# A Fourier filter and a gated feed-forward on one core: the buffer `at` of two batches laid out by halves, and small copies moved to GpSimd

## The chip, the cores and the metric

The kernel runs on one core of a Trainium2 chip. A core has engines that each work through their own queue in order: TensorE (PE, its weight loads PEld), VectorE (DVE), ScalarE (ACT), GpSimd (POOL) and SyncE (SP, which only issues transfers). They meet through semaphores. SBUF is the on-chip memory of 128 partitions; PSUM, eight banks here, takes TensorE's results; DMA queues move data between SBUF and DRAM. The metric is the device time of the program in microseconds. Before the change it is 893.33 us, the median of three runs (893.03 to 893.96).

## The reference

Eight batches of a sequence of 3008 positions by 256 channels pass a global filter in the Fourier domain, and then a feed-forward with a product of two branches:

```
X = rfft(x, axis=1)                      # x: (8, 3008, 256)
y = irfft(X * (filt_r + 1j*filt_i), n=3008, axis=1)
t = y.reshape(24064, 256)
out = (relu(t @ w_gate) * (t @ w_val)) @ w_out    # d_ff = 1536, out: (24064, 256)
```

Inputs and output are float32. The kernel uses bf16 for most matmuls.

## The kernel before

The length is split as 3008 = 94 x 32, a position being 32 n1 + n2. The transform is made of matmuls in four stages for each batch.

Stage A is the transform over n1 (94 points, real input). For batches 0 and 1 `first_a` multiplies x (`XF`, float32) by the matrix `WA`, and ScalarE copies the result out of PSUM as bf16, in two halves h of the 256 channels. What is now indexed by frequency on the partitions and n2 along the row must be turned so that n2 lies on the partitions. `turn_a` does that with VectorE's transpose of 32 x 32 blocks, on pairs of bf16 taken as float32, and writes the buffer `ats[b]` (`at` in the profile). Batch 0 is turned in two pieces of 128x2048 float32, one for each half h. Of batch 1, half 0 goes another way: `store_half` writes it to DRAM (`Abuf`) and `load_half` reads it back, turned, with four DMAs of SP's queue into channels 0 to 127 of `at`. Half 1 is turned by VectorE in four smaller pieces of 128x512. Batches 2 to 7 take other functions (`fold_chunk` on GpSimd, `tiled_a`, `load_at_tiled`).

Stage B is the transform over n2, the filter, and the way back: `fwd` (TensorE, `F2` with `at`, into `psX`), `product` (VectorE, for some of batch 0 ScalarE's copy `xs` and then GpSimd; `tt` with the real filter `Ftr`, `uu` with the imaginary filter `Fti`), `inv` (TensorE with the tables `I2t` and `I2u`, into `psD`). For batch 0 the result goes back into `AS0`, the buffer that held stage A's result, now called D: rows 0 to 23 of its 32 rows. `turn_d` transposes all 32 rows into `dCb`. Other batches write D to DRAM (`Dbuf`).

Stage C is the transform back over k1: `item_c` multiplies `dCb` by the table `M1` (`M` in the profile) into `psY`, which is copied to `yT`, a block of 512 tokens. Rows of `M1` that answer to D's spare columns are zero.

Stage D is the feed-forward, 47 blocks of 12 steps. A step (`gv`) makes `psV` and `psG` with two matmuls each, ScalarE copies `psV` to `vsb`, VectorE makes `prod` from `psG` and `vsb`; `o_part` multiplies the products of the block before by `WoT` into `psO`. From the second block on, each step also holds four matmuls of `o_part`. Every `psV`, `psG`, `psY` takes a bank from one list of eight, in the program's order; a bank is free when its reader is done.

The order on each engine is written out by hand: each engine runs its instructions as the program lists them. Work for later batches is hung on the steps with `at_step`: batch 1's remaining `turn_a` pieces at steps 4, 11 and 14, its first `fwd` at step 16, the loads of x of batch 2 from step 6. Waits are derived from the areas of memory that instructions read and write. The first `turn_a` piece of batch 1, `turn_a(1, 1, 0, 0, 16)`, stands before the first block, and so before the first `prod` on VectorE.

`place_own` writes parts of three tables from the loaded array `tabs`: the last two groups of `I2t` and `I2u` in the upper 64 partitions, and `M1`. `place_filter` copies rows of the filters to the partitions above, seven times by SP's DMA and once by GpSimd (`Fti`, 32x3072). GpSimd issues the loads of filters and of the feed-forward's weights (`load_vg`, `load_o`).

Of the kernel before, what the change touches and what calls it, by code (L numbers as in the profile page):

```python
# [12 lines left out]
FP32 = mybir.dt.float32  # L13
BF16 = mybir.dt.bfloat16
# [17 lines left out]
NG = 24  # L32
# [3 lines left out]
def _ap(t, offset_elems, ap_list):  # L36
    return dataclasses.replace(
        t, offset=t.offset + offset_elems, ap=[list(p) for p in ap_list]
    )
# [80 lines left out]
def kernel(  # L120
# [10 lines left out]
    nc = tc.nc  # L131
    B, S_, D = x.shape
# [15 lines left out]
    sb = ctx.enter_context(tc.tile_pool(name="sb", bufs=2))  # L148
# [3 lines left out]
    def bank(name, *shape):  # L152

        i = free.pop(0)
        t = ps.tile([128, *shape], FP32, tag=f"bank{i}", bufs=1, name=name)
        held[id(t)] = i, t
        return t
# [13 lines left out]
    AS0 = pro.tile([128, 32, D], BF16)  # L171
# [4 lines left out]
    M1 = consts.tile([128, 2, N1], BF16)  # L176
# [22 lines left out]
    tabs = pro.tile([128, tab_h.shape[1]], BF16, tag="tabs", bufs=1)  # L199
# [23 lines left out]
    def place_own():  # L223

        for i, t in enumerate((I2t, I2u)):
            o = 192 + i * 128
            nc.vector.tensor_copy(t[64:, NG - 2:, :],
                                  tabs[64:, o:o + 128].rearrange("p (g n) -> p g n", g=2))
        nc.vector.tensor_copy(M1, tabs[:, 448:].rearrange("p (l n) -> p l n", l=2))

    nyq = []

# [19 lines left out]
    def place_filter(fi, a, half, copy):  # L252

        dst = FILT[fi][1]
        gs = slice(H * half, H * half + H)
        r = a * 64
        copy(dst[r + 32:r + 64, gs, :], dst[r:r + 32, gs, :])
# [5 lines left out]
    def load_vg(c0, c1):  # L263
        for (w_hbm, w_sb) in ((moe_w_val, WvT), (moe_w_gate, WgT)):
            nc.gpsimd.dma_start(w_sb[:, :, c0:c1],
                                _ap(w_hbm, c0, [[DFF, 128], [128 * DFF, 2], [1, c1 - c0]]))

    def load_o():
        for c in range(2):
            nh = NFT // 2  # L270
            nc.gpsimd.dma_start(WoT[:, c * nh:(c + 1) * nh],
                                _ap(moe_w_out, c * nh * 128 * D, [[D, 128], [128 * D, nh], [1, D]]))
# [22 lines left out]
    def turn_a(b, h, i=0, d0=0, d1=None):  # L295

        src = AS[2 * b + h][i].rearrange("p l c d -> p (l c) d").bitcast(FP32).rearrange("p n d -> p d n")
        w = src.shape[1]
        d1 = d1 or w
        dst = ats[b].bitcast(FP32).rearrange("p k d -> p d k")  # L300
        o = h * D // 4 + i * w
        nc.vector.transpose(dst[:, o + d0:o + d1, :], src[:, d0:d1, :])

    def new_at(b):
        ats[b] = sb.tile([128, 32, D], BF16, tag="at", bufs=1, name="at")

    def turn_d(h):

        src = AS0.bitcast(FP32).rearrange("p k d -> p d k")
        dst = dCb[:, 0:32, :].bitcast(FP32).rearrange("p n d -> p d n")  # L310
        d = slice(h * D // 4, h * D // 4 + D // 4)
        nc.vector.transpose(dst[:, d, :], src[:, d, :])
# [7 lines left out]
    def load_half(b):  # L320
        w = N2 * D // 2
        for q in range(4):
            nc.sync.dma_start(ats[b][32 * q:32 * q + 32, 0:NG, 0:D // 2],
                              _ap(Abuf[b], q * NG * w, [[D // 2, 32], [w, NG], [1, D // 2]]))

    fold = {}
# [56 lines left out]
    ats = {}  # L383
# [4 lines left out]
    def fwd(b, i):  # L388

        for e in range(2):  # L390
            psXs[b, i, e] = bank("psX", 2, D)
            left[b, i, e] = 2
        for m in range(2):
            for e in range(2):
                for a in range(2):
                    j = 12 * a + 2 * i + m
                    nc.tensor.matmul(psXs[b, i, e][64 * a:64 * a + 64, m],  # L397
                                     F2[64 * e:64 * e + 64, j, :],
                                     ats[b][64 * e:64 * e + 64, j, :], start=True, stop=True,
                                     tile_position=(64 * e, 64 * a))  # L400

    def product(b, i, e, k, pool=False):

# [42 lines left out]
    def first_b(amid):  # L446

        for i in range(6):
            fwd(0, i)
            on_pool = [(i, e) in POOL_U for e in range(2)]  # L450
            seq = {(0, 0): ((0, 0), (0, 1), (1, 0), (1, 1)), (0, 1): ((1, 1), (0, 0), (0, 1), (1, 0)),
                   (1, 0): ((0, 1), (1, 0), (1, 1), (0, 0)), (1, 1): ((0, 0), (1, 1), (0, 1), (1, 0))}
            for e, k in seq[tuple(map(int, on_pool))]:
                product(0, i, e, k, pool=k == 1 and on_pool[e])
            if i > 1:
                inv(0, i - 2)
            amid(i)
        inv(0, 4)
        amid(6)
        inv(0, 5)  # L460
# [107 lines left out]
    q = NX2 * D // 4  # L568
# [29 lines left out]
    for i in range(3):  # L598
        make_back_u(i)
    new_at(0)  # L600
    for h in range(2):
        turn_a(0, h)
    place_own()
    for i in range(6):
        warm(2)
    place_filter(1, 0, 0, nc.gpsimd.tensor_copy)
    nc.gpsimd.memset(AS0[:, NG:, :], 0.0)
    for fi, a, half in ((0, 0, 0), (0, 1, 0), (1, 1, 0), (0, 0, 1), (0, 1, 1), (1, 0, 1), (1, 1, 1)):
        place_filter(fi, a, half, nc.sync.dma_start)
    load_x(1, sp, ((0, 0, 2 * q), (0, 2 * q, 4 * q), (1, 0, 2 * q), (1, 2 * q, 4 * q)))  # L610
# [11 lines left out]
    load_vg(0, DFF // 2)  # L622
    load_vg(DFF // 2, DFF)
    load_o()
    for h in range(2):
        turn_d(h)
    new_at(1)
    for p, s, h in items:
        first_a(1, p, s, h)
        if (p, s, h) == (3, 1, 0):  # L630
            store_half(1)
            load_half(1)
        if (p, s, h) == (3, 0, 1):
            for hh in range(2):
                item_c(0, hh)
    turn_a(1, 1, 0, 0, 16)
    nc.sync.dma_start(WF, nc.inline_tensor(fold_h, name="dft_fold").ap())
    prologue.close()
# [8 lines left out]
    for k in range(1, 4):  # L647
        at_step((4, 11, 14)[k - 1], lambda k=k: turn_a(1, 1, k // 2, k % 2 * 16, k % 2 * 16 + 16))
    for b in range(1, B):
        end = (b * S // W - 1) * NFT + C_AT[0] - 5  # L650
        if b > 1:
            for j, e in enumerate((-74, -69, -64, -57)):
                l = (6, 14, 22, 30)[j] if b == 2 else end - 115 + NFT * j

                def next_x(b=b, j=j, l=l):
                    hold_gpsimd(prods[-1][:, 0:8])
                    load_chunk(b, j)
                    if j:
                        fold_chunk(b, j - 1)
                    if j == 3:  # L660
                        fold_chunk(b, j)
                at_step(l, next_x)
                at_step(end + e, lambda b=b, j=j: tiled_a(b, j))
            at_step(end + e + 4, lambda b=b: load_at_tiled(b))
        for i in range(7):
            l = -35 + 5 * i if b == 1 else -40 + 6 * i
            if i < 6:
                at_step(end + l, lambda b=b, i=i: fwd(b, i))
                for h in range(4):
                    at_step(end + l + h, lambda b=b, i=i, h=h: product(b, i, h // 2, h % 2))  # L670
            if i > 0:
                at_step(end + l, lambda b=b, i=i: inv(b, i - 1))
        at_step(end - 2, lambda b=b: load_d(b))
# [42 lines left out]
```

## Time and profile before

| | |
|---|---|
| Median of three runs | 893.33 us |
| The profiled execution's own time | 893.89 us |
| Its span, first to last instruction | 892.1 us |
| TensorE busy | 866.5 us, 97% of the span |
| VectorE, ScalarE, GpSimd busy | 65%, 56%, 41% |
| Mean granted TensorE clock | 0.994 |
| Moved by DMA | 102.87 MB, mean 115 GB/s |

A profile row of the order of time reads: start in us from the span's first instruction, duration in us, engine, line, operation, out<-in, shapes, number of merged instructions, and in brackets the idle time of the engine before it and what ended that. A row of waits reads: who waited for whom, us in total, times, the longest. A row of groups has count, busy us and mean ns. Matmuls overlap, so their starts tell more than their durations. A DMA's landing is told from its issue. The granted clock is a share of TensorE's full clock.

### The profile page before, as it was taken

To read this page: it belongs to the slowest core of one execution; us is meant where nothing else is said; L and a number is where in the kernel's file an instruction comes from. 1 tells how busy PE (TensorE), PEld (TensorE's weight loads), DVE (VectorE), ACT (ScalarE), POOL (GpSimd) and SP (SyncE) were. 2 spreads that over 40 slices of the span, in tenths; PEclk is the share of its full clock that TensorE was granted. 3 is DMA by queue.
4 is the path that set the end of the run, shared out by engine and by line. 5 is a ranking of instruction groups with operands and counts; after the bars stand their busy time and mean duration, and the time that the engine had idled before them with its cause. 6 is when DMAs were issued, how large, how long until landed. Compare 5 with 4: busy or idle time off the path is not lost.

```text
span 892.1 us, 19099 instructions
## 1 busy us (share of the span) xinstructions
PE 866.5 (97%) x7072; PEld 509.0 (57%) x7193; DVE 579.6 (65%) x864; ACT 501.3 (56%) x905; POOL 365.3 (41%) x365
## 2 busy tenths in 40 slices
PE   8869999999999999999999999999999999999997
PEld 4325555566556665566655566556655566666665
DVE  3847766577665776667766677657776577655553
ACT  5644655556655556555655556555665555555553
POOL 6805980038841488216690167802886000000001
PEclk9989999999999999999999999999999999999999
DMA  9893436534466436463375434763456513331111
GB/s 242 226 160 95 108 102 154 122 86 124 129 143 134 115 100 144 128 142 93 100 174 130 103 100 108 184 125 89 116 142 148 121 30 82 84 72 36 37 31 53
DMA packets 107075, 102.87 MB, mean 115 GB/s; under 512 B 24215, under 2 KB 92343, under 8 KB 106214
## 3 DMA queue, kind: packets, MB, share of 16 engines
q1 hardware_dynamic: 83974, 74.45, 34.6%
q0 software_dynamic: 22608, 26.41, 12.5%
q8 instruction: 57, 0.93, 0.5%
q10 hardware_dynamic: 400, 0.79, 0.3%
q14 instruction: 36, 0.29, 0.1%
HBM read 58.16 MB, written 45.88 MB: 117 GB/s over the span
## 4 chain that ended last, share of the span: by engine, by line
PE 89%; DMA 4%; DVE 2%; ACT 1%; issue 1%; POOL 1%; SPq 0%; DVEq 0%; POOLq 0%
PE psG L509 28%; PE psO L530 26%; PE psV L509 25%; PE psF L360 3%; PE psD L428 2%; PE psY L492 2%; PE psX L397 2%; DVE prod L514 2%; ACT vsb L512 1%; DMA at<-Abuf 1%; PE psA L285 1%; DMA Fti<-in_filt_i_dram 1%; DMA XF<-in_x_dram 1%; DMA Abuf<-dCb 1%; DMA Fti<-Fti 1%
## 5 line engine op out<-in xcount | busy, mean ns | idle before, releaser
L514 DVE SCALAR_TENSOR_TENSOR prod<-psG,vsb 128x512 bf16<-128x512 f32 x564 | 388.8, 690 | 257.2 <-ACT vsb L512 250.7
L512 ACT CAST vsb<-psV 128x512 bf16<-128x512 f32 x564 | 332.2, 589 | 272.9 <-PE psV L509 213.0
L509 PE MATMUL psG<-yT,WgT 128*128 128x512 bf16 x1107 | 332.5, 380 | 12.6 <-DVE prod L514 7.4
L530 PE MATMUL psO<-WoT,prod 128*128 128x256 bf16 x2256 | 336.5, 273 | 1.1
L509 PE MATMUL psV<-yT,WvT 128*128 128x512 bf16 x1030 | 316.9, 381 | 0.9 <-DVE yT L500 0.6
L530 PEld LDWEIGHTS <-prod 128*128 128x128 bf16 x2256 | 220.7, 98 | 143.3
L509 PEld LDWEIGHTS <-WgT 128*128 128x128 bf16 x1128 | 110.4, 98 | 143.0 <-issue 10.8
L277 POOL CAST scr<-prod 128x8 f32<-128x8 bf16 x24 | 4.6, 192 | 299.1 <-DVE prod L514 273.7
L509 PEld LDWEIGHTS <-WvT 128*128 128x128 bf16 x1128 | 98.7, 98 | 42.5 <-issue 32.3
L554 POOL DMA_DIRECT2D out_dram<-osb x5 | 2.6, 538 | 200.0 <-ACT osb L543 200.0
L543 ACT COPY osb<-psO 128x512 f32<-128x512 f32 x92 | 54.0, 586 | 25.8 <-PE psO L530 24.0
L413 DVE TENSOR_TENSOR tt<-psX,Ftr 128x512 bf16<-128x512 f32 x96 | 64.9, 681 | 0.7 <-ACT xs L410 0.3
L413 DVE TENSOR_TENSOR uu<-psX,Fti 128x512 bf16<-128x512 f32 x88 | 59.9, 681 | 0.0
L333 POOL DMA_DIRECT2D XF<-in_x_dram x96 | 56.9, 597 | 3.3 <-PE psY L492 1.5
L346 POOL TENSOR_TENSOR fold<-XF 128x1024 f32<-128x1024 f32 x24 | 57.2, 2384 | 0.7
L347 POOL TENSOR_TENSOR XF<-XF 128x1024 f32<-128x1024 f32 x24 | 56.5, 2352 | 1.9
L438 ACT CAST dsb<-psD 128x512 bf16<-128x512 f32 x84 | 45.1, 589 | 10.9 <-PE psD L428 10.9
L367 DVE CAST asb<-psF 128x512 bf16<-128x512 f32 x48 | 30.9, 686 | 17.8 <-PE psF L360 17.8
L367 ACT CAST asb<-psF 128x512 bf16<-128x512 f32 x48 | 25.8, 589 | 29.0 <-PE psF L360 29.0
L498 ACT CAST yT<-psY 128x512 bf16<-128x512 f32 x47 | 27.6, 586 | 23.0 <-PE psY L492 22.9
L492 PE MATMUL psY<-M,dCb 96*128 96x94 bf16 (+19 forms) x604 | 37.5, 198 | 0.0
L492 PEld LDWEIGHTS <-dCb 96*128 96x128 bf16 (+1 forms) x604 | 34.5, 97 | 3.3 <-issue 0.8
(70 smaller groups left out, 477.2 us busy)
## 6 DMA issues: line engine op xcount, KB each, us to landing
XF<-in_x_dram POOLq DMA_DIRECT2D x48, 256.0 KB, 6.1
Dbuf<-dsb SPq DMA_DIRECT2D x84, 128.0 KB
dCb<-Dbuf SPq DMA_DIRECT2D x56, 192.0 KB
XF<-in_x_dram POOLq DMA_DIRECT2D x96, 96.0 KB, 2.7
Abuf<-asb SPq DMA_DIRECT2D x96, 96.0 KB
at<-Abuf SPq DMA_DIRECT2D x24, 384.0 KB
out_dram<-osb SPq DMA_DIRECT2D x69, 94.0 KB
XF<-in_x_dram SPq DMA_DIRECT2D x20, 256.0 KB
```

The costliest lines, as they stand in the source:

```text
L333: nc.gpsimd.dma_start(xp[r:r + 24, 0:4:2, :], _ap(x, (b * N1 * N2 + o) * D, [[N2 * D, 24], [47 * N2 * D, 2], [1, 512]]))
L346: tt(t, xp[:, 0:2], xp[:, 2:4], op=ALU.add)
L347: tt(xp[:, 2:4], xp[:, 0:2], xp[:, 2:4], op=ALU.subtract)
L367: copy(asf[:, :, q, :], banks[q])
L413: nc.vector.tensor_tensor(p, psX, filt, op=ALU.mult)
L438: copy(dsb[:, a, o:o + 2, :] if b else AS0[:, 12 * a + 2 * i:12 * a + 2 * i + 2, :], psD[a])
L492: nc.tensor.matmul(psY[:, o:o + w], dCs[b, n2 // 8][:, n2 % 8, h * 128:(h + 1) * 128], M1[:, 1, n1:n1 + w] if b == 0 else M1[:NROW, 0, n1: ...
L509: nc.tensor.matmul(pt[:, :W], w[:, h, ft * 128:(ft + 1) * 128], yt[:, h, :], start=(h == 0), stop=(h == 1))
L512: nc.scalar.copy(vsb, psV[:, :W])
L514: nc.vector.scalar_tensor_tensor(prod, in0=psG[:, :W], scalar=0.0, in1=vsb, op0=ALU.max, op1=ALU.mult)
L530: nc.tensor.matmul(psO[:, t % 2], prods[ft][:, t * 128:(t + 1) * 128], WoT[:, ft, :], start=(ft == 0), stop=(ft == NFT - 1))
L543: copy(osb[:, t0 % 2:t % 2 + 1], psO[:, t0 % 2:t % 2 + 1])
```

## The change

Four things change.

- `ats[b]` of batches 0 and 1 has the shape 128 x 2 x 32 x 128 in place of 128 x 32 x 256: the half of the channels comes before the row. `turn_a` and `load_half` write one half each; `fwd` reads a row's 256 channels as two runs of 128. The buffer of later batches keeps its shape.
- `place_own` copies its parts of `I2t` and `I2u` with GpSimd in place of VectorE. In the program's order it stays ahead of GpSimd's `place_filter` of `Fti`.
- The copy of `M1` leaves `place_own`; GpSimd does it after issuing the weight loads.
- The clearing of `AS0[:, 24:32, :]` by GpSimd goes. D's spare columns hold what stage A left there, finite numbers that meet zero rows of `M1`.

```
         for i, t in enumerate((I2t, I2u)):
             o = 192 + i * 128
-            nc.vector.tensor_copy(t[64:, NG - 2:, :],
+            nc.gpsimd.tensor_copy(t[64:, NG - 2:, :],
                                   tabs[64:, o:o + 128].rearrange("p (g n) -> p g n", g=2))
-        nc.vector.tensor_copy(M1, tabs[:, 448:].rearrange("p (l n) -> p l n", l=2))
...
-        dst = ats[b].bitcast(FP32).rearrange("p k d -> p d k")
-        o = h * D // 4 + i * w
+        dst = ats[b][:, h].bitcast(FP32).rearrange("p k d -> p d k")
+        o = i * w
         nc.vector.transpose(dst[:, o + d0:o + d1, :], src[:, d0:d1, :])
...
-        ats[b] = sb.tile([128, 32, D], BF16, tag="at", bufs=1, name="at")
+        ats[b] = sb.tile([128, 2, 32, D // 2], BF16, tag="at", bufs=1, name="at")
...
-            nc.sync.dma_start(ats[b][32 * q:32 * q + 32, 0:NG, 0:D // 2],
+            nc.sync.dma_start(ats[b][32 * q:32 * q + 32, 0, 0:NG, :],
                               _ap(Abuf[b], q * NG * w, [[D // 2, 32], [w, NG], [1, D // 2]]))
...
-                                     ats[b][64 * e:64 * e + 64, j, :], start=True, stop=True,
-                                     tile_position=(64 * e, 64 * a))
+                                     ats[b][64 * e:64 * e + 64, j, :] if b > 1 else ats[b][64 * e:64 * e + 64, :, j, :],
+                                     start=True, stop=True, tile_position=(64 * e, 64 * a))
...
     place_filter(1, 0, 0, nc.gpsimd.tensor_copy)
-    nc.gpsimd.memset(AS0[:, NG:, :], 0.0)
...
     load_o()
+    nc.gpsimd.tensor_copy(M1, tabs[:, 448:].rearrange("p (l n) -> p l n", l=2))
```

## The prediction

> **What bounds the kernel now.** I read the page's first two parts, then the table by stretches, then the waits and the order of time around the stretch that stood out.
>
> ```profile
> PE 866.5 (97%) x7072; PEld 509.0 (57%) x7193; DVE 579.6 (65%) x864; ACT 501.3 (56%) x905; POOL 365.3 (41%) x365
> PEclk9989999999999999999999999999999999999999
> ```
>
> TensorE is the bound over the whole span. A change pays only where TensorE stands idle or runs slowly, and the granted clock drops in one slice of forty, the third (44.6 to 66.9 us). The stretches around it (length, busy time of PE, PEld, DVE, ACT, POOL, granted clock, DMA share, GB/s):
>
> ```profile
> 53.00:57.00 4.00, 3.95 (x18) 1.76 (x18) 0.01 (x1) 2.31 (x5) 0.00 (x0) 1.00 1.35 206
> 57.00:64.50 7.50, 0.12 (x1) 0.00 (x0) 1.76 (x3) 0.00 (x0) 0.00 (x0) 0.70 0.72 105
> 64.50:70.00 5.50, 5.47 (x13) 1.87 (x13) 4.72 (x7) 2.50 (x5) 0.12 (x1) 0.50 0.02 3
> 200.00:892.00 692.00, 682.18 (x5652) 408.63 (x5740) 448.78 (x687) 389.62 (x696) 269.62 (x254) 1.00 0.44 107
> ```
>
> From 57.0 to 64.5 nearly everything stands still, and then TensorE works 5.5 us at half clock. After 200 us it is busy 98.6% of the time at full clock. Who waited between 50 and 75 us:
>
> ```profile
> DVE at L302 <- DMA at<-Abuf: 9.7, 1, 9.7
> ACT vsb L512 <- DVE prod L514: 8.5, 1, 8.5
> PE psG L509 <- DVE prod L514: 7.4, 1, 7.4
> ```
>
> The three are one chain. A VectorE transpose of `turn_a` waits for the DMA of `load_half`; the products of the first block stand behind it in VectorE's queue; TensorE finds no free PSUM bank. In order of time, on VectorE:
>
> ```profile
> 52.32 0.69 DVE L500 CAST yT<-psY 128x512 bf16<-128x512 f32 x1 [2.83 <-PE psY L492]
> 62.73 1.19 DVE L302 STREAM_TRANSPOSE at<-asb 128x512 f32<-128x512 f32 x1 [9.72 <-DMA at<-Abuf]
> 63.83 3.04 DVE L514 SCALAR_TENSOR_TENSOR prod<-psG,vsb 128x512 bf16<-128x512 f32 x5
> ```
>
> and on TensorE:
>
> ```profile
> 53.07 0.59 PE L509 MATMUL psV<-yT,WvT 128*128 128x512 bf16 x2
> ...
> 54.80 0.59 PE L509 MATMUL psV<-yT,WvT 128*128 128x512 bf16 x2
> ...
> 56.52 0.59 PE L509 MATMUL psV<-yT,WvT 128*128 128x512 bf16 x2
> 64.53 1.01 PE L509 MATMUL psG<-yT,WgT 128*128 128x512 bf16 x2 [7.41 <-DVE prod L514]
> ...
> 71.20 0.39 PE L492 MATMUL psY<-M,dCb 128*128 128x52 bf16 x6
> ...
> 75.53 0.60 PE L530 MATMUL psO<-WoT,prod 128*128 128x256 bf16 x4
> ...
> 81.26 0.41 PE L397 MATMUL psX<-at,F 64*64 64x256 bf16 x8
> ```
>
> **Part 1: the buffer by halves.** Before, the transpose writes columns D/2 to D of every row of `at` while the DMA writes columns 0 to D/2 of the same rows: no element is shared, but the two areas interleave. After, each half is one stretch of a partition. In the order of the changed kernel's instructions this transpose waits for ScalarE alone; TensorE's first read of `at` at line 397 already carries its own waits for the DMA, so nobody reads early. The same order shows what is added: the first product now waits for the DMA that brought `tabs`, which VectorE's copies of it had waited for (they run at 26.0, below), and the first `psY` and `vsb` wait for GpSimd's copy of `M1`. The first is met 25 us before; the second is costed in part 2. Behind the first stand all products, and so TensorE.
>
> What the wait costs: a step starts every 0.865 us (53.07 and, two steps on, 54.80), and the `psY` at 71.20 comes after nine. At that pace it would come at 53.07 + 7.79 = 60.86. The loss is **10.3 us**: 7.4 of idle time and the rest half clock. The lower bound is 7.4, if the slow clock stayed for another reason; the upper one is 10.8, with some of the later small waits for `yT`.
>
> What is late next? VectorE now waits for ScalarE's last `asb` copy:
>
> ```profile
> 53.27 0.65 ACT L292 CAST asb<-psA 128x256 bf16<-128x256 f32 x2 [0.28 <-PE psA L285]
> 53.82 0.59 ACT L512 CAST vsb<-psV 128x512 bf16<-128x512 f32 x1
> ```
>
> The half that it needs is the first of the two, done near 53.65. The transpose ends at 53.65 + 1.19 = 54.85, the first product near 55.5; `psG` of step 4, which stalled, is due at 56.95. The products follow 0.61 us apart (3.04/5), TensorE's steps 0.865, so VectorE catches up even with the next 1.19 us transpose at step 4. The DMA loses its cover of waiting and must be there for line 397: 81.26 − 10.3 = 71.0, against a landing by 62.7: 8 us to spare. The output weights are needed at 75.53 − 10.3 = 65.2:
>
> ```profile
> WoT<-in_moe_w_out_dram POOLq DMA_DIRECT2D x2, 384.0 KB, 14.3
> ```
> ```profile
> 42.76 1.67 POOL L271 DMA_DIRECT2D WoT<-in_moe_w_out_dram  x2
> ```
>
> Issued from 42.76 to 44.4 and landing 14.3 us after the issue in the median, they are there near 58 to 59. The chunk loads of batch 2 leave POOL some 10 us earlier too, after product 6 near 61, when the half load is about over.
>
> **The address pattern.** The two transposes of batch 0 now write 32-row columns at a step of 256 bytes, not 512; the load's runs stay at 256 bytes. Rows (count, then busy, mean ns):
>
> ```profile
> L302 DVE STREAM_TRANSPOSE at<-AS 128x2048 f32<-128x2048 f32 x2 | 8.3, 4214 | 12.7 <-ACT AS L292 12.7
> L312 DVE STREAM_TRANSPOSE dCb<-AS 128x2048 f32<-128x2048 f32 x2 | 7.3, 3718 | 0.1
> ```
>
> The first reads at 256 and writes at 512 bytes; the second does both at 512. So steps may matter by 0.5 us each, in either direction: −1.0 to +1.0 for the two, and I take 0, as the source step stays. TensorE reads the two halves as two runs of 128 in one matmul; 96 matmuls are concerned, 0.05 us apart (0.41 per eight), and I take 0; doubled they would cost 4.8, of which only the batch 0 half has no other work between.
>
> **Part 2: copies to GpSimd, the clearing dropped.**
>
> ```profile
> 26.00 0.19 DVE L227 COPY I2t<-tabs 64x128 bf16<-64x128 bf16 x1
> 26.11 1.87 DVE L227 COPY I2u<-tabs 64x128 bf16<-64x128 bf16 x1
> 28.00 1.21 DVE L229 COPY M<-tabs 128x188 bf16<-128x188 bf16 x1
> 29.12 0.68 DVE L413 TENSOR_TENSOR tt<-psX,Ftr 128x512 bf16<-128x512 f32 x1
> 29.72 0.68 DVE L413 TENSOR_TENSOR uu<-psX,Fti 128x512 bf16<-128x512 f32 x1
> ```
> ```profile
> 21.92 2.74 POOL L257 COPY Fti<-Fti 32x3072 bf16<-32x3072 bf16 x1
> 26.09 1.85 POOL L607 MEMSET AS<- 128x2048 bf16 x1 [1.43 <-DVE at L302]
> 27.99 2.26 POOL L411 TENSOR_TENSOR uu<-xs,Fti 128x512 bf16<-128x512 f32 x2
> ...
> 37.67 2.27 POOL L411 TENSOR_TENSOR uu<-xs,Fti 128x512 bf16<-128x512 f32 x2
> ```
>
> Two copies of one size take 0.19 and 1.87 us; the long one ends with the clearing (27.98 and 27.94), and `M` ends with the first GpSimd product. VectorE is held while GpSimd works. So 3.1 us go from VectorE's path (26.0 to 29.12), and 1.85 from GpSimd's. But GpSimd now does the two small copies ahead of `Fti`, and the second waits for ScalarE:
>
> ```profile
> 22.54 1.65 ACT L220 CAST I2u<-psI 128x512 bf16<-128x512 f32 x3
> ```
>
> It starts at 24.2, takes 0.2 to 0.4, and the 2.74 us copy ends at 27.3, not 24.66.
>
> ```profile
> 26.02 0.41 PE L397 MATMUL psX<-at,F 64*64 64x256 bf16 x8 [0.29 <-DVE at L302]
> ```
>
> VectorE's first `tt` can run at 26.5, when `psX` is there; its `uu` needs `Fti` and runs at 27.35, not 29.72; GpSimd's first product at 27.35, not 27.99, and its third, which waited for VectorE, 2.3 earlier. The products gain **2.3 us**. `M` is copied after the weight loads (44.43 − 2.3), near 42.1, and first read at 51.65 (below) less at most 2.3; 7 us cover it, and without them it costs the 0.2 to 1.2 of the copies above.
>
> How much reaches the end? TensorE's transform of batch 1 reads x as it lands:
>
> ```profile
> 41.25 10.57 PE L285 MATMUL psA<-XF,WA 128*128 128x512 f32 x24
> 51.65 0.63 PE L492 MATMUL psY<-M,dCb 128*128 128x94 bf16 x12
> ```
> ```profile
> q1 hardware_dynamic: 12, 0.04, 6.5%
> ```
>
> The last row is x's queue between 40 and 42 us, its last 12 packets; from 42 to 44 it has none. The last quarter of x is first read by the seventh matmul, at 41.25 + 6 × 0.44 = 43.9, so 1.9 us, less a few tenths for the landing, of the 2.3 fit before x is late: 1.5. And the weight loads, which leave POOL after its last product (37.67 + 2.27 = 39.94), come 2.3 us earlier, into the tail of x. If they stretch that tail by half its 2 us, 0.5 remains; if it doubles, nothing, or a loss of 0.5. I take −0.9, between 0.5 and 1.5; ends −2.3 and +0.5, or +1.5 with the slower transposes.
>
> **Sum.** −10.3 − 0.9 = −11.2 on the profiled execution's 893.89 gives 882.7; it stands 0.56 above the median, 893.33, so I forecast **882.1**.
>
> **The rivals.**
> - A: x is late. The weights double the tail of x or the transposes slow down; part 2 loses 0.5 to 1.5: about 884.0. For: 12 packets of x come as late as 40 to 42. Against: 1.5 us of slack. Chance 0.15.
> - B: VectorE's transposes hold GpSimd as GpSimd held VectorE's copies. Then the small copies start when the transposes end, at 26.0, `Fti` ends at 29.1, `uu` runs at 29.15, 0.6 earlier than before, and the end is 893.3 − 10.3 − 0.6 = 882.4, inside the forecast's own range. Against: the `Fti` copy ran during a transpose at 2.74/3072 = 0.89 ns an element, the clearing at 1.85/2048 = 0.90 with none. Chance 0.08. [...]
> - C: another wait takes half of the stall: VectorE lags behind steps 4 to 11, or the half load comes late. 5 us of 10.3 return: 887. Chance 0.07.
> - D: the wait stays, as on the whole tile; 0.9 remains: 892.4. Chance 0.02.
> - E, slower: the new step of 256 bytes is a bad one for the transposes. It decides from 4.2 + 11.2/2 = 9.8 us each; at three times 4.2 the two cost 16.9 more on a path where nothing covers them: 899. The two rows differ by 13% only. Chance 0.04.
>
> **How the numbers follow.** 0.64 for the forecast, with its own range 880.3 to 883.5. 0.2% is 1.8 us, about what a measurement of this kernel tells from no change; A, B, C and the forecast are faster (0.94), D is the same (0.02), E slower (0.04). The range runs from 880.0 (10.8 and 2.3, rounded) to 885.0, which takes in A and leaves C, D and E out.
>
> **What would show it.** Right: no idle stretch of TensorE over 2 us from 53 to 70 and clock 1.00 there; the transpose starts near 53; the first `tt` near 26.5, and `Fti`'s copy on GpSimd ends near 27.3. Wrong: a VectorE wait for `at<-Abuf`, TensorE waiting for x before 44 by more than 2 us, or transposes well over 4.2 us.

## The result and the profile after

The changed kernel takes **880.75 us**, the median of four runs (880.46 to 880.93), against 893.64 (893.03 to 893.99) for the kernel before on the same chip: a ratio of 0.9856, interval 0.9839 to 0.9873. The forecast was 882.1, with a range of 880.0 to 885.0. The profiled execution took 880.93 us with a span of 879.1, so 12.96 us less than the 893.89 of the one before.

The page of the changed kernel, busy time by engine and the granted clock in 40 slices:

```profile
PE 869.7 (99%) x7193; PEld 508.1 (58%) x7193; DVE 576.5 (66%) x861; ACT 501.3 (57%) x905; POOL 364.3 (41%) x367
PEclk9999999999999999999999999999999999999999
```

The slice of lower clock is gone, and TensorE is busy 99% of the span. The same stretches as before (length, busy time of PE, PEld, DVE, ACT, POOL, clock, DMA share, GB/s):

```profile
53.00:57.00 4.00, 4.00 (x21) 1.79 (x19) 3.65 (x6) 2.62 (x6) 0.00 (x0) 1.00 1.36 187
57.00:64.50 7.50, 7.25 (x47) 3.71 (x46) 6.94 (x11) 4.74 (x9) 3.97 (x7) 1.00 0.73 122
64.50:70.00 5.50, 5.50 (x41) 3.06 (x40) 4.44 (x7) 2.20 (x5) 2.77 (x6) 1.00 0.44 125
```

From 57.0 to 64.5 TensorE works 7.25 us in place of 0.12. Of the waits of 50 to 75 us, the transpose's 9.7 for the DMA has become 0.7 for ScalarE, and the only one left on TensorE's side is short:

```profile
DVE at L301 <- ACT asb L291: 0.7, 1, 0.7
PE psV L508 <- DVE yT L499: 0.3, 1, 0.3
```

VectorE in order of time, from batch 0's turning to the first products of the feed-forward:

```profile
17.87 8.29 DVE L301 STREAM_TRANSPOSE at<-AS 128x2048 f32<-128x2048 f32 x2 [12.87 <-ACT AS L291]
26.66 0.69 DVE L412 TENSOR_TENSOR tt<-psX,Ftr 128x512 bf16<-128x512 f32 x1 [0.50 <-PE psX L396]
27.57 0.69 DVE L412 TENSOR_TENSOR uu<-psX,Fti 128x512 bf16<-128x512 f32 x1 [0.21 <-POOL Fti L256]
...
51.53 1.21 DVE L301 STREAM_TRANSPOSE at<-asb 128x512 f32<-128x512 f32 x1 [0.66 <-ACT asb L291]
52.64 1.96 DVE L513 SCALAR_TENSOR_TENSOR prod<-psG,vsb 128x512 bf16<-128x512 f32 x3
```

and SP's queue in the same execution:

```profile
50.65 5.43 SPq L322 DMA_DIRECT2D at<-Abuf  x4
```

So the transpose does not merely find the load finished; it no longer waits for it. The last of the four DMAs is issued at 53.0 (this issue takes until 56.08), when the transpose has already ended (51.53 + 1.21 = 52.74).

GpSimd of the changed kernel:

```profile
23.48 0.29 POOL L227 COPY I2t<-tabs 64x128 bf16<-64x128 bf16 x1 [2.63 <-issue]
24.46 0.29 POOL L227 COPY I2u<-tabs 64x128 bf16<-64x128 bf16 x1 [0.69 <-ACT I2u L220]
24.79 2.74 POOL L256 COPY Fti<-Fti 32x3072 bf16<-32x3072 bf16 x1
27.62 2.27 POOL L410 TENSOR_TENSOR uu<-xs,Fti 128x512 bf16<-128x512 f32 x2
```

TensorE of the changed kernel, and behind it the last `psV` of the kernel before (its other rows stand in the prediction):

```profile
26.21 0.41 PE L396 MATMUL psX<-at,F 64*64 64x256 bf16 x8 [0.27 <-DVE at L301]
...
39.11 10.57 PE L284 MATMUL psA<-XF,WA 128*128 128x512 f32 x24
...
50.93 0.59 PE L508 MATMUL psV<-yT,WvT 128*128 128x512 bf16 x2
...
58.70 0.39 PE L491 MATMUL psY<-M,dCb 128*128 128x52 bf16 x6
...
68.76 0.41 PE L396 MATMUL psX<-at,F 64*64 64x256 bf16 x8
...
868.27 0.59 PE L508 MATMUL psV<-yT,WvT 128*128 128x512 bf16 x2
```

```profile
880.78 0.59 PE L509 MATMUL psV<-yT,WvT 128*128 128x512 bf16 x2
```

Four rows of TensorE cut an execution into stretches: first `psX`, first `psV`, the `psY` after nine steps, last `psV`. The moment of the first `psX` itself lies between 25.8 and 27.9 us in the profiles of this study, without regard to the edit, and moves everything behind it; so the comparisons below go by the lengths between these rows. The column after the first `psX` has an uncertainty of its own: two further profiles of the changed kernel gave 24.66 and 24.74, a second one of the kernel with the copies on VectorE 24.62. A difference of 0.2 in it decides nothing.

| Profiled kernel | first psX | psX to psV | psV to the psY after nine steps | first to last psV |
|---|---|---|---|---|
| before | 26.02 | 27.05 | 18.13 | 827.71 |
| after | 26.21 | 24.72 | 7.77 | 817.34 |
| layout alone | 26.83 | 27.12 | 7.77 | 817.34 |
| copies and clearing alone | 27.32 | 24.73 | 18.45 | 828.04 |
| before, pieces at steps 12 to 15 | 27.50 | 27.06 | 7.77 | 818.93 |
| before, 34 idle matmuls | 25.82 | 27.09 | 16.23 | 825.80 |
| after, with the clearing | 26.17 | 26.27 | 7.77 | 817.35 |
| after, copies on VectorE | 25.99 | 24.41 | 7.77 | 817.35 |
| after, Fti first | 26.82 | 24.41 | 7.77 | 817.36 |

From before to after: the start +0.19, the stretch to the first `psV` −2.33, the feed-forward −10.37, and from the last `psV` to the end of the span 11.32 became 10.83, −0.49; outside the span +0.04. Together −12.96, the whole difference.

### The profile page after: what moved, and what is told of

The parts are those of the page before. It is cut to its first block, busy times and chain, and to the rows that moved or that the text cites. A ratio compares the mean times of both kernels' runs of the same rounds, so it can differ in the third digit from the quotient of the medians.

```text
span 879.1 us, 19217 instructions
## 1 busy us (share of the span) xinstructions
PE 869.7 (99%) x7193; PEld 508.1 (58%) x7193; DVE 576.5 (66%) x861; ACT 501.3 (57%) x905; POOL 364.3 (41%) x367
## 4 chain that ended last, share of the span: by engine, by line
PE 96%; POOL 1%; ACT 1%; DMA 1%; DVE 1%; issue 0%; SPq 0%; POOLq 0%
PE psV L508 29%; PE psG L508 28%; PE psO L529 27%; PE psA L284 3%; PE psF L359 3%; PE psY L491 2%; PE psD L427 2%; PE psX L396 2%; DMA XF<-in_x_dram 0%; POOL out_dram L553 0%; POOL Fti L256 0%; POOL uu L410 0%; DMA out_dram<-XF 0%; ACT I2t L213 0%; ACT I2u L220 0%
## 5 line engine op out<-in xcount | busy, mean ns | idle before, releaser
L508 PE MATMUL psV<-yT,WvT 128*128 128x512 bf16 x1128 | 336.7, 379 | 0.6 <-DVE yT L499 0.6
L542 ACT COPY osb<-psO 128x512 f32<-128x512 f32 x92 | 54.0, 586 | 25.8 <-PE psO L529 24.0
L366 ACT CAST asb<-psF 128x512 bf16<-128x512 f32 x48 | 25.8, 589 | 29.0 <-PE psF L359 29.0
```

The lines of the kernel that those rows point to most:

```text
L366: copy(asf[:, :, q, :], banks[q])
L508: nc.tensor.matmul(pt[:, :W], w[:, h, ft * 128:(ft + 1) * 128], yt[:, h, :], start=(h == 0), stop=(h == 1))
L542: copy(osb[:, t0 % 2:t % 2 + 1], psO[:, t0 % 2:t % 2 + 1])
```

## The experiments

**1. The layout alone.** The changed kernel with the three copies on VectorE and the clearing on GpSimd, as before:

```
-            nc.gpsimd.tensor_copy(t[64:, NG - 2:, :],
+            nc.vector.tensor_copy(t[64:, NG - 2:, :],
...
+        nc.vector.tensor_copy(M1, tabs[:, 448:]...)
...
+    nc.gpsimd.memset(AS0[:, NG:, :], 0.0)
...
-    nc.gpsimd.tensor_copy(M1, tabs[:, 448:]...)
```

> The layout by halves alone; the copies stay on VectorE and the clearing stays. Theory: the false wait of the transpose is worth 10.4 us and nothing else changes, so 893.6 - 10.4 = 883.3, and the first block starts near 53.1 us as before. If the layout also changed the transposes or the matmuls of stage B, the first block would start more than 0.5 us earlier or later than 53.1.

Measured: 884.06 (883.81 to 884.39), 0.8 above the number expected; ratio 0.9891, interval 0.9874 to 0.9907. TensorE's rows of this kernel:

```profile
53.95 0.59 PE L509 MATMUL psV<-yT,WvT 128*128 128x512 bf16 x2
...
61.72 0.39 PE L492 MATMUL psY<-M,dCb 128*128 128x52 bf16 x6
```

The nine steps take 7.77, as after the whole change, and the stretch from the first `psX` to the first `psV` is that of before (27.12). The layout removes the stall, all of it, and changes nothing else in these lengths. The profiled execution (884.18) began 0.81 later than that of the kernel before (26.83 against 26.02), which is as much as the miss; whether the other runs did so too is not known.

**2. Copies and clearing alone.** The kernel before with the other edits:

```
-            nc.vector.tensor_copy(t[64:, NG - 2:, :],
+            nc.gpsimd.tensor_copy(t[64:, NG - 2:, :],
...
-        nc.vector.tensor_copy(M1, tabs[:, 448:]...)
...
-    nc.gpsimd.memset(AS0[:, NG:, :], 0.0)
...
+    nc.gpsimd.tensor_copy(M1, tabs[:, 448:]...)
```

> The copies on GpSimd and the dropped clearing alone; the old layout stays. Theory: the first block starts 2.1 us earlier (near 51) as in the changed kernel, the stall stays and moves along with the load, so 893.6 - 2.1 = 891.5. Rival, as predicted: x lands late and caps the gain at 0.9, so 892.7, with TensorE waiting for x near 42 to 44 us; then the 2.1 of the changed kernel came from an early landing of x in that program alone.

Measured: 890.95 (889.50 to 893.31), ratio 0.9972, interval 0.9963 to 0.9981. From the first `psX` to the first `psV` it takes 24.73, 2.32 less than before: all that the products gain. No wait for x stands there, and the rival's 892.7 is out. The profiled execution, at 893.31, was the slowest of the ten; it began 1.30 later than that of the kernel before (27.32 against 26.02) and its stall was 0.32 longer, so only the stretch is compared. The medians of the two single edits are 9.6 and 2.7 below their 893.67; together 12.3, of a change that gives 12.9.

**3. The old layout, its transposes out of the way.** Is it the layout itself that matters, or only that a waiting transpose stands ahead of the products? Here the layout is that of before, the DMA and the transposes still wait for one another, but all four pieces come when the load has landed:

```
-    turn_a(1, 1, 0, 0, 16)
...
-    for k in range(1, 4):
-        at_step((4, 11, 14)[k - 1], lambda k=k: turn_a(...))
+    for k in range(4):
+        at_step(12 + k, lambda k=k: turn_a(...))
```

> The kernel before with the old layout; only the four transposes of batch 1's half 1 are hung on steps 12 to 15 of the blocks in place of before step 0 and at steps 4, 11 and 14. The wait for the load stays in the program but is over when VectorE reaches it. Theory (the queue behind the waiting transpose is what cost time): 883.3 to 884.5, the last 1 us for four transposes packed in four steps. Rival (the layout itself makes the difference): no change, 893.6.

Measured: 885.84 (885.48 to 886.31), ratio 0.9911, interval 0.9896 to 0.9926. The order of time of this kernel, TensorE and then VectorE:

```profile
54.56 0.59 PE L509 MATMUL psV<-yT,WvT 128*128 128x512 bf16 x2
...
62.33 0.39 PE L492 MATMUL psY<-M,dCb 128*128 128x52 bf16 x6
...
73.88 0.51 PE L397 MATMUL psX<-at,F 64*64 64x256 bf16 x8 [1.41 <-DVE at L302]
```

```profile
67.66 1.20 DVE L302 STREAM_TRANSPOSE at<-asb 128x512 f32<-128x512 f32 x1
...
72.63 1.19 DVE L302 STREAM_TRANSPOSE at<-asb 128x512 f32<-128x512 f32 x1
```

The stall is gone here too: 7.77 for nine steps. So the price was that of a queue: one transpose waiting in front of products that waited for nothing. What the late place costs is seen at 73.88, where the first `psX` of batch 1 waits 1.41 for the last transpose; from the first to the last `psV` it takes 1.59 more than with the new layout (818.93 against 817.34). The median lies 1.3 above the expected range and 1.8 above that of the layout alone (884.06). The layout gives the transposes an early place without that delay.

**4. The half clock by itself.** Of the 10.3 us the prediction put 7.4 on idle time and the rest on the half clock behind it. Matmuls that nobody reads, in the idle time of the kernel before, keep TensorE busy; its wait stays. First 40 of them:

```
+    psJ = bank("psJ", 512)
...
+            if (k, ft) == (0, 3):
+                for _ in range(40):
+                    nc.tensor.matmul(psJ, WvT[:, 0, 0:128], WvT[:, 0, 0:512], start=True, stop=True)
+                done(psJ)
```

> The kernel before with 40 matmuls of 512 columns into a PSUM bank of their own, which nobody reads, put before step 3 of the first block, where TensorE would stand idle: 40 x 0.215 = 8.6 us. The wait stays. Theory: the granted clock stays at 1.00, the half-clock stretch after the stall goes, and the time falls by 2.6 to 2.9 us to 891.0. Rival (VectorE's backlog, not the clock, sets the pace after the stall): 893.6 or more.

Measured: 892.87 (892.03 to 894.68), ratio 0.9992, interval 0.9983 to 1.0002. This decides nothing: the idle matmuls outlasted the wait, and in the profiled execution the clock was low at another place (last section). So once more with 34:

> The kernel before with 34 matmuls that nobody reads, in place of 40, ahead of step 3 of the first block. With 40 TensorE came 1.06 us late to the wait's end (the first psG of step 4, taken against each kernel's own first vsb), and from there to the psY it saved 2.79 us. Theory (after its idle stretch TensorE runs at half clock, which costs 2.6 to 2.9 us of the 10.3): 34 cover the wait to within 0.3 us, clock 1.00 throughout, 890.8 to 891.2. Rival (the products on VectorE set the pace after the wait, the clock costs nothing): 893.6.

Measured: 891.58 (891.40 to 894.22), ratio 0.9982, interval 0.9973 to 0.9991. The table by stretches of the kernel with 34, and TensorE in order of time:

```profile
57.00:64.50 7.50, 6.87 (x32) 3.04 (x31) 1.47 (x2) 0.00 (x0) 0.00 (x0) 1.00 0.74 103
64.50:70.00 5.50, 5.18 (x29) 2.47 (x29) 5.50 (x10) 3.94 (x7) 0.19 (x1) 1.00 0.00 1
```

```profile
55.50 7.50 PE L681 MATMUL psJ<-WvT 128*128 128x512 bf16 x34
...
64.82 0.59 PE L509 MATMUL psV<-yT,WvT 128*128 128x512 bf16 x2 [0.96 <-DVE prod L514]
65.25 0.59 PE L509 MATMUL psG<-yT,WgT 128*128 128x512 bf16 x2
...
69.14 0.40 PE L492 MATMUL psY<-M,dCb 128*128 128x52 bf16 x6
```

The clock is 1.00 where it was 0.50. From the `psG` of step 4 to the `psY` it takes 69.14 − 65.25 = 3.89, against 71.20 − 64.53 = 6.67 before: the half clock cost **2.78 us**, and the products on VectorE could follow the faster pace, so the rival falls. Of the 2.78, 1.91 arrive between first and last `psV` (825.80 against 827.71), since `psG` of step 4 comes 0.88 later than before, counted from the first `psV` (65.25 − 52.91, the first `psV` of this profile, is 12.34; 64.53 − 53.07 is 11.46). About half of this, 0.43, is one more pair of matmuls behind the wait: the idle matmuls hold one of the eight banks, so that already `psV` of step 4 waits (0.96). The other half is the wait itself, which in this execution ended 0.45 later after the first `psV` (64.82 − 52.91 = 11.91). The median, 2.2 below its 893.76, is less than expected by this.

**5. Which part of part 2 does it?** Three kernels beside a second sample of the changed one:

> The changed kernel once more, as the base of the three runs beside it: 880.8, the ratio to the kernel before within 0.985 to 0.987.

It gave 881.31 (881.16 to 881.44), ratio 0.9858 (0.9840 to 0.9876): 0.5 above the time expected, the ratio inside its range.

The clearing back in its place on GpSimd, behind the `Fti` copy:

```
     place_filter(1, 0, 0, nc.gpsimd.tensor_copy)
+    nc.gpsimd.memset(AS0[:, NG:, :], 0.0)
```

> The changed kernel with the clearing put back on GpSimd behind the Fti copy. Theory (the whole GpSimd time ahead of its products counts): its products start 1.85 us later, near 29.4 in place of 27.6, and the third one ends about 1.5 to 1.85 later; the first vsb comes that much later, 882.3 to 882.6. Rival (the gain lies in VectorE's earlier tt and uu alone): the first vsb stays where it is and the time is 880.8.

Measured: 882.66 (882.57 to 882.88), 1.35 more than the changed kernel beside it. GpSimd of this kernel:

```profile
27.59 1.80 POOL L606 MEMSET AS<- 128x2048 bf16 x1
29.44 6.72 POOL L410 TENSOR_TENSOR uu<-xs,Fti 128x512 bf16<-128x512 f32 x6
```

Its products start at 29.44 in place of 27.62, and the stretch to the first `psV` grows from 24.72 to 26.27. GpSimd's time ahead of its products is on the path.

No clearing, but all three copies back on VectorE:

```
-            nc.gpsimd.tensor_copy(t[64:, NG - 2:, :],
+            nc.vector.tensor_copy(t[64:, NG - 2:, :],
...
+        nc.vector.tensor_copy(M1, tabs[:, 448:]...)
...
-    nc.gpsimd.tensor_copy(M1, tabs[:, 448:]...)
```

> The changed kernel with the three small copies back on VectorE, and still no clearing. Theory (they were long only because GpSimd held VectorE during the clearing and the first product): the two table copies take 0.2 to 0.3 us each, the Fti copy on GpSimd ends near 24.7, tt runs near 26.6 to 27.2 and GpSimd's first product near 26.5; the third copy may be held for up to 2.3 us by that product, and where it is, VectorE's tt is late by as much and the kernel loses up to 2. So 880.5 to 881.3 if it is not held, 882 to 883 if it is. Rival (the copies are slow on VectorE by themselves): 1.2 to 1.9 us each, tt near 29, time 883.1.

Measured: 880.91 (880.60 to 881.26), ratio 0.9854, interval 0.9838 to 0.9869. VectorE of this kernel:

```profile
25.97 0.19 DVE L227 COPY I2t<-tabs 64x128 bf16<-64x128 bf16 x1
26.08 0.19 DVE L227 COPY I2u<-tabs 64x128 bf16<-64x128 bf16 x1
26.28 0.21 DVE L229 COPY M<-tabs 128x188 bf16<-128x188 bf16 x1
```

With GpSimd at rest (its `Fti` copy ends at 23.40, its first product starts at 27.20) the same copies take 0.19, 0.19 and 0.21, not 0.19, 1.87 and 1.21. They were never slow by themselves. With the new layout, dropping the clearing alone gives the whole of part 2; where the copies are placed then makes no difference that can be measured. What holds the copies while GpSimd works is not shown. It does not hold all that VectorE does: in the kernel before, `tt` took 0.68 (29.12 to 29.80) while GpSimd's second product ran, which ended at 30.25.

`Fti` copied ahead of the two table copies, all on GpSimd:

```
-    place_own()
     for i in range(6):
         warm(2)
     place_filter(1, 0, 0, nc.gpsimd.tensor_copy)
+    place_own()
```

> The changed kernel with the Fti copy ahead of the two small table copies on GpSimd. Theory: Fti is there near 24.7, the two small copies end near 25.4, before the transposes end; uu no longer waits 0.21 us and GpSimd's first product starts near 26.5 or as soon as its own data are there, up to 1.1 earlier than 27.62. Up to 1.1 us less than the changed kernel, 879.7 to 880.8. Rival (the start of the products is set by x or by the transposes alone): 880.8.

Measured: 881.33 (881.09 to 881.48), no difference to the changed kernel beside it, as the rival says. VectorE's `uu` no longer waits, but GpSimd's first product then waits for ScalarE's copy `xs`:

```profile
28.03 6.92 POOL L410 TENSOR_TENSOR uu<-xs,Fti 128x512 bf16<-128x512 f32 x6 [2.76 <-ACT xs L409]
```

That is 1.21 after the first `psX` (26.82), against 1.41 in the changed kernel (27.62 − 26.21): up to 0.2 is there to gain, not 1.1.

**6. Is x the next limit?** The prediction took part 2 at less than the products gain because x would come late. Six small loads, read by nobody, delay the issue of x's last quarter in the changed kernel:

```
+    late = consts.tile([32, 6, 64], FP32)
...
-    load_x(1, sp, ((0, 0, 2 * q), (0, 2 * q, 4 * q), (1, 0, 2 * q), (1, 2 * q, 4 * q)))
+    load_x(1, sp, ((0, 0, 2 * q), (0, 2 * q, 4 * q), (1, 0, 2 * q)))
+    for i in range(6):
+        nc.sync.dma_start(late[:, i, :], ...)
+    load_x(1, sp, ((1, 2 * q, 4 * q),))
```

> The changed kernel with six small loads, read by nobody, on the same queue ahead of the last quarter of batch 1's x: at some 0.63 us for each issue that quarter is issued 3.8 us later and lands near 45.0, where TensorE first reads it near 41.8. Theory (x has 0.6 to 1.1 us to spare in the changed kernel and then bounds it): TensorE waits 2.7 to 3.2 us there and the kernel takes 883.8 to 884.4. Rival (something else has more slack behind it, so x does not bound): 881.3.

Measured: 883.45 (882.18 to 888.74), ratio 0.9901, interval 0.9879 to 0.9924, between the two expectations. The profiled execution took 882.31; its SP queue and TensorE:

```profile
33.47 3.11 SPq L611 DMA_DIRECT2D late<-in_x_dram  x6
36.97 2.12 SPq L193 DMA_DIRECT2D XF<-in_x_dram  x3
```

```profile
40.67 10.57 PE L285 MATMUL psA<-XF,WA 128*128 128x512 f32 x24
```

The loads took 0.52 us each, not 0.63, and this execution began late (first `psX` at 27.86), so that x was there in time all the same: the run of 24 matmuls takes 10.57 as ever, and 24.63 lie between first `psX` and first `psV`. The other runs of it spread over 6 us, which the changed kernel's do not, but none of those was profiled. How late x must be to bound stays open.

**7. VectorE or GpSimd for the copies, once more.** The same kernel as in 5, beside another sample of the changed one:

> The kernel with the halves, all small copies on VectorE and no clearing once more, beside a second run of the changed kernel: from the first psX to the first vsb it took 25.16 us against 25.41 of the changed kernel, so 0.25 less, 880.6 to 881.1 against 880.8 to 881.3. Rival: the two are the same.

> The changed kernel once more, beside the run above: 880.8 to 881.3.

Measured: 881.41 (880.93 to 881.53) and 881.22 (880.65 to 881.49). They are the same; the 0.4 between them in 5 did not come again. No version tried here beats the changed kernel by more than its measurement is uncertain.

The profile of this sample with the copies on VectorE also bears on what experiment 6 left open. SP's queue, then TensorE, then x's queue from 40 to 42 (packets, megabytes, share):

```profile
28.94 7.56 SPq L192 DMA_DIRECT2D XF<-in_x_dram  x12
```

```profile
26.70 0.41 PE L397 MATMUL psX<-at,F 64*64 64x256 bf16 x8 [0.31 <-DVE at L302]
...
39.50 10.57 PE L285 MATMUL psA<-XF,WA 128*128 128x512 f32 x24
...
51.32 0.59 PE L509 MATMUL psV<-yT,WvT 128*128 128x512 bf16 x2
```

```profile
q1 hardware_dynamic: 20, 0.07, 8.1%
```

Here x is issued as late as before the change (28.94, 28.89), and TensorE comes to its 24 matmuls 1.75 earlier than then (39.50, 41.25). 20 packets still arrive from 40 to 42, and by 42, near the seventh matmul (39.50 + 6 × 0.44 = 42.1), x is there. The 24 matmuls take their 10.57 all the same, and from the first `psX` to the first `psV` it takes 24.62, 0.21 more than in this kernel's other profile. So with x as late as before the change and TensorE 1.75 earlier, x costs 0.2 at most.

## Why the prediction was right, and where it was off

**Part 1, 10.3 us: right, mechanism and size.** The `psY` after nine steps was put at the first `psV` plus 7.79; it came at plus 7.77. From first to last `psV` the gain is 10.37. The transpose waits for ScalarE alone and ends at 52.7 (51.53 + 1.21), 1.8 after the first `psV`, as worked out (54.85 against 53.07). The layout alone gives the same 10.37, and taking the waiting transpose out of VectorE's queue ends the stall without any new layout, so it was the queue that passed the wait on. That the new layout takes the wait itself away is seen in SP's queue: the transpose ended before the last DMA of the load was issued. The split is measured as well: 2.78 for the half clock, and so some 7.6 for idle time.

**What is late next: right.** The `psX` of batch 1 comes at 68.76 and waits for nothing; the 0.25 for a `yT` is all that is left there.

**The address pattern, taken as 0: right.** The two transposes took 8.29, against 8.31 for the pair before:

```profile
17.66 8.31 DVE L302 STREAM_TRANSPOSE at<-AS 128x2048 f32<-128x2048 f32 x2 [12.66 <-ACT AS L292]
```

TensorE's rows of eight `psX` matmuls, which now read two runs of 128, take 0.41 as before (26.21 and 26.02). Rival E is out.

**Part 2: the products' gain of 2.3 right, what reaches the end wrong.** The `Fti` copy ends at 27.53 (27.3 was worked out), `tt` starts at 26.66 (26.5), `uu` at 27.57 (27.35), GpSimd's products at 27.62 (27.35). The step that failed is "I take −0.9, between 0.5 and 1.5": all 2.33 arrived at the first `psV`, and 2.32 with the copies and the clearing alone. Taking less than 2.3 rested on x's last packets, seen at 40 to 42 us in one execution. But the moment at which SP issues x's loads differs between executions. The order of time of SP's queue, before and then after, and third the packets, megabytes and share of x's queue in the changed kernel, from 38 to 40 and from 40 to 42:

```profile
28.89 7.56 SPq L192 DMA_DIRECT2D XF<-in_x_dram  x12
```

```profile
27.65 7.56 SPq L192 DMA_DIRECT2D XF<-in_x_dram  x12
```

```profile
q1 hardware_dynamic: 58, 0.26, 33.2%
...
q1 hardware_dynamic: 1, 0.00, 0.0%
```

1.24 us earlier, with one packet left after 40 in place of 12, although the program of SP's queue is the same. In the fourteen profiles the loads start between 26.5 and 28.94; the execution on which the prediction rested had the latest but one. Nor is there a sign that the weight loads, issued from 37.75 in place of 39.89, held up x's tail: 12.35 us after the first issue one packet was left. The term had been lowered in two steps. The one for the weights, from 1.5 to 0.9, was made for a tail that did not stretch: also with x issued as late as before, in experiment 7, it was there by 42. The other, from 2.3 to 1.5, assumes that x's margin of 1.9 is used up, and no profile came so far: where TensorE was 2.14 earlier (39.11 against 41.25), x was earlier too, and where x was late, TensorE was 1.75 earlier. So rival A did not happen in any profile; that x would bind by some tenths if both came together is not refuted.

**The other rivals.** B is out: the table copy ran on GpSimd at 23.48 in 0.29 us, in the middle of VectorE's transposes (17.87 to 26.16), and did not wait for their end. C and D are out by the stretch from 57 to 70, with clock 1.00 and 0.25 us idle.

**The sum.** Forecast −11.2 on the profiled execution, measured −12.96. Part 2 was 1.4 too small, and the rest, −0.3, is the start (+0.19) and the tail (−0.49), which vary between executions: 11.24 from the last `psV` to the end of the span in the second profile of the changed kernel (879.6 − 868.36).

## What to carry to other kernels

When a stall is long, look at what stands first in the waiting engine's queue, and ask whether that instruction needs the data or only shares a stretch of memory with them; laying the two areas apart, or moving the instruction back, ended the same stall, and cost nothing or 1.6 us. Price the idle time and the half clock behind it together (some 7.6 and 2.78 us here). A landing time read from one execution is a sample: a term that rests on a margin of 1 to 2 us to a DMA gets a wider range, not a smaller value.

## What the runs showed of the hardware

**The clock can drop at a stretch where the same program otherwise keeps it.** Up to its idle matmuls at 58 us the kernel with 40 of them runs what the kernel before runs. The table by stretches of its profile, and then of the kernel before:

```profile
32.00:34.00 2.00, 2.00 (x18) 0.83 (x17) 2.00 (x4) 1.31 (x3) 0.82 (x1) 0.50 0.78 274
34.00:38.00 4.00, 4.00 (x45) 1.93 (x48) 2.34 (x5) 3.02 (x7) 3.94 (x5) 0.50 0.98 350
```

```profile
32.00:34.00 2.00, 1.31 (x25) 0.60 (x24) 2.00 (x5) 1.82 (x5) 1.71 (x2) 1.00 0.77 238
34.00:38.00 4.00, 3.61 (x58) 1.69 (x53) 3.32 (x7) 4.00 (x9) 3.85 (x6) 1.00 0.98 346
```

The same sparse stretch was granted 0.50 in one execution and 1.00 in the other, and the first `psV` came 28.32 after the first `psX` in place of 27.05, 1.27 us later. Read in windows of half a microsecond, five of the fourteen profiles have a stretch of half clock in their first 80 us:

| Profiled kernel | where | half clock, us | length |
|---|---|---|---|
| before | long stall | 59.97 to 70.21 | 10.24 |
| copies and clearing alone | long stall | 59.23 to 69.47 | 10.24 |
| before, 40 idle matmuls | sparse stretch | 31.22 to 38.04 | 6.82 |
| before, 34 idle matmuls | sparse stretch | 31.06 to 34.47 | 3.41 |
| layout alone | sparse stretch | 31.91 to 35.32 | 3.41 |

The lengths are one, two and three times 3.41 us. The two of 3.41 cost next to nothing (27.09 and 27.12 from the first `psX` to the first `psV`, against 27.05); the one of 6.82 goes with the 1.27. The sparse stretch fell to half clock in three of the five profiles that keep the clearing and the copies of the kernel before, and in none of the nine others. What decides which execution loses the clock, no run here shows. In the long stall of the kernel before, the clock was halved 2.9 us after the last matmul had ended (57.11), and for the last 5.7 us of the half clock TensorE was at work again (64.53 to 70.21).

**The start of the program varies from one execution to the next.** The first `psX` came between 25.82 and 27.86 us in fourteen profiled executions, with the same work ahead of it but for small copies. Ahead of it TensorE waits for x, 0.99 us in the profile of the kernel before (first `psX` at 26.02) and 0.31 in that of the changed one (26.21), where another 1.04 pass without a wait that the profile shows; what makes the whole difference was not followed. A difference of 1 us between two profiles means little before this is taken off. Lengths between rows of one engine repeat better: the nine steps take 7.77 in all ten profiles without the stall, and first to last `psV` takes 817.34 to 817.36 in the nine of them with the new layout.
